# Memory attention and an erf-softplus FFN on one core: ScalarE's softplus and erf in groups of four steps, a first unit in float32, and a later split of w_out

## The chip, the cores and the metric

The kernel runs on one core of one Trainium2 chip. The metric is the device time of one execution in microseconds; lower is better. PE is TensorE, PEld its weight loads, DVE is VectorE, ACT is ScalarE, POOL is GpSimd, and SP's queue issues the transfers.

## The reference, cut to what matters

```python
# q, k, v: 8 batches x 8 heads x 576 tokens x 64; phi: 8 x 8 x 576 x 32
a = softmax(phi, axis=2)                    # over the 576 tokens
k_m = einsum('bhsm,bhsd->bhmd', a, k)       # 32 memories a head
v_m = einsum('bhsm,bhsd->bhmd', a, v)
attn = softmax(q @ k_m.T / 8, axis=-1) @ v_m
x = attn.transpose(0, 2, 1, 3).reshape(4608, 512)
h = x @ w_in                                # 512 -> 2048
sp = maximum(h, 0) + log1p(exp(-abs(h)))    # softplus
g = h * erf(sp)
return g @ w_out                            # 2048 -> 512
```

All inputs are float32. q, k and phi are scaled up, so that both softmaxes are sharp.

## The kernel before, in words

A **unit** is 288 tokens of one batch, half of its 576; there are 16. d_ff is cut into 8 **chunks** `c` of 256. A **step** `i` is one chunk of one unit, `u, c = divmod(i, 8)`: 128 steps.

The attention output is never formed. `kmvm(b, g)` makes k_m and v_m of four heads on PE, `block_diag` turns them into `km` and `vm`, and `vw(b, c)` multiplies v_m of all heads into chunk c of w_in, once per batch. `scores(u)` gives the scores, `sm_max`, `sm_norm` and `sm_back` their softmax, and `ffn1(i, j)` multiplies the attention weights `at` by the `vw` chunk, 288 tokens by 128 columns of h for each j in 0 and 1. `ffn2(i, d)` adds g of the step, times w_out's two blocks, into four accumulators `pso` of 128 columns of the output.

**Products.** Both operands of `ffn1` and `ffn2` are split into an fp32r high part and an fp32r rest (`split`: ACT copies, DVE subtracts), and three matmuls are made for each product, high x high, high x rest, rest x high (`products`). A step is 12 matmuls of `ffn1` (L390) and 24 of `ffn2` (L437), all 128 x 128 by 288.

**Activation.** h x erf(softplus(h)) is formed from Tanh alone. ACT takes `tt = tanh(0.5 h + GB)` for each j (L397), DVE multiplies (1 + tt) by h into `acc` (L398), and then `factor(i, n)` for n = 0, 1, 2 takes a Square or a Tanh of `tt` on ACT (L411, L413) and multiplies it into `acc` on DVE (L414). `g_split` makes g_hi on ACT (L422) and g_lo on DVE (L423). All functions in it, and Exp, are in one activation table.

**Weights.** w_in and w_out come as float64 bits. A piece is decoded by `decode_1` (DVE clamps, L142; ACT scales two times, L145 and L146) and `decode_2` (two passes of DVE, L159 and L162). For w_out `decode_3` splits too: ACT copies the high part (L174), PE subtracts it from the F32 value by two matmuls with the identity and its negative (L177, L178), ACT copies the rest out of PSUM (L179). Six of the eight chunks of each weight are pieces of 1 MB, the last two are pieces of half that. The decoded w_in stays in SBUF in F32, as every batch needs it for `vw`.

**Order.** `prog` is a list of calls. In front of the loop stand the first batch's attention and `LEAD` = 7 pieces of decoding. Slot i of the main loop issues `ffn1(i, 0)`, `factor(i-1, 1)`, `ffn1(i, 1)`, and then, merged, `factor(i-1, 2)`, `factor(i, 0)`, `g_split(i-2)`, the four `ffn2(i-3, d)` and the tasks in `side[i]`: in the first eight slots the decoding of two more pieces each and `vw(0, i+1)`, and everywhere the next units' and batches' attention (`unit_tasks`, `batch_tasks`), with `vw_pair` in four slots of each 16. A scheduler that simulates the engines orders each engine's instructions from this list; on DVE an instruction may not pass the one 28 places ahead of it in the list (`WINDOW`).

**Loads.** `queue` holds the loads in the order in which the program needs them; each belongs to a kind with so much `room` (buffers), `frees` gives room back, and `FIRST` sets the order of the first ones on SP's queue:

```python
FIRST = "wo phiT start phi wo raw raw wo raw start wo q".split()
```

`wo` stands for a 1 MB weight piece (in slots of the same pool as the split w_out), `raw` for k and v of a pair of heads (four transfers) or a half piece, `start` for a first-batch load in a borrowed buffer.

**Buffers.** PSUM: two for h (`ps_h`), four accumulators (`ps_o`), two for everything else (`ps_a`). SBUF: `tt` 2, `acc` 3, `f` 3, g_hi and g_lo 3 each.

Of the kernel before, what the change touches and what calls it, by code (L numbers as in the profile page):

```python
# [8 lines left out]
F32 = mybir.dt.float32  # L9
# [16 lines left out]


GC, GB = 0.27160413, -0.45239282
FACTORS = (
    ("Q", -1.75972316, 0.52065829),  # L30
    ("T", 0.56841178, 1.0199725, 0.42607248),
    ("T", 1.35008185, -1.89147316, 1.73987114),
)
# [3 lines left out]
def tile_memory_attention_then_erf_softplus_ffn(  # L37
# [3 lines left out]
    k: bass.AP,  # L41
    v: bass.AP,
# [7 lines left out]
    P = 128  # L50
    B, _, S = qT.shape
    H = k.shape[2]
# [12 lines left out]
    NF = len(FACTORS)  # L65
    SC = [(c * P, min(P, S - c * P)) for c in range((S + P - 1) // P)]
    RAW_BUFS = 3
    STAGED = 6
    FIRST = "wo phiT start phi wo raw raw wo raw start wo q".split()
    LEAD = 7  # L70
    WINDOW = {mybir.EngineType.DVE: (12, 28)}
    PO = 5
    SO = 2
    VL = 4
    VB = 1
# [18 lines left out]
    minus = const.tile([P, P], F32R, name="minus")  # L94
    nc.scalar.activation(minus, ident, AF.Identity, scale=-1.0)
# [3 lines left out]
    def column(value, name):  # L99
        t = const.tile([P, 1], F32, name=name)  # L100
        nc.vector.memset(t, value)
        return t

    tb = column(GB, "tb")
    fb = [column(f[1] if f[0] == "Q" else f[2], f"fb{i}") for i, f in enumerate(FACTORS)]
    fd = [f[2] if f[0] == "Q" else f[3] for f in FACTORS]

    w_in_sb = {}
    wo = {}

# [9 lines left out]
    def load_weight(*key):  # L120
        name, c, r, n = key
        if n == NP_:
            t = wop.tile([P, NP_ * 256], I64, name="w_" + name, tag="wo")
        else:
            t = raw_pool.tile([P, n * 256], I64, name="raw")
        if name == "in":
            nc.sync.dma_start(
                out=t.rearrange("p (r f) -> p r f", r=n),
                in_=w_in[:, r : r + n, c * 256 : (c + 1) * 256],
            )  # L130
        else:
            nc.sync.dma_start(
                out=t.rearrange("p (r d) -> p r d", d=DM),
                in_=w_out[:, 2 * c + r : 2 * c + r + n // 2],
            )
        st[key] = t
# [11 lines left out]
    def decode_2(*key):  # L148
        name, c, r, n = key
        v = st[key].bitcast(I32).rearrange("p (n two) -> p n two", two=2)  # L150
        lo, hi = v[:, :, 0], v[:, :, 1]
        dst = hi
        if name == "in":
            if r == 0:
                if c % 2 == 0:
                    w_in_sb[c // 2] = const.tile([P, NP_, 512], F32, name=f"w_in{c // 2}")
            dst = w_in_sb[c // 2].bitcast(I32)[:, r : r + n, c % 2 * 256 : (c % 2 + 1) * 256]
            hi, lo = (x.rearrange("p (r f) -> p r f", f=256) for x in (hi, lo))
        nc.vector.scalar_tensor_tensor(  # L159
# [3 lines left out]
            out=dst, in0=hi, scalar=-(2**31), in1=lo, op0=ALU.bitwise_and, op1=ALU.bitwise_or  # L163
        )

    def decode_3(*key):
        name, c, r, n = key
        t = st.pop(key)
        if name == "out":
            w = t.bitcast(F32).rearrange("p (r d two) -> p r d two", d=DM, two=2)[:, :, :, 1]  # L170
            if r == 0:
                wo[c] = wop.tile([P, 2, 2, DM], F32R, name="wo", tag="wo")
            hi, lo = (wo[c][:, x, r : r + n // 2] for x in range(2))
            nc.scalar.activation(hi, w, AF.Identity)  # L174
            for x in range(n // 2):
                ps = ps_a.tile([P, DM], F32, name="psa")
                nc.tensor.matmul(out=ps, lhsT=ident, rhs=w[:, x], start=True, stop=False)  # L177
# [11 lines left out]
    def load_phi(b):  # L189
# [6 lines left out]
        if ln < P:  # L196
            nc.sync.dma_start(out=t[:ln, n], in_=phi[b, s0 : s0 + ln])
# [446 lines left out]
```

## Time and profile before

| | |
|---|---|
| runs | 788.66, 788.80 (median), 789.77 us |
| profiled execution | 790.4 us, of which the span of the instructions is 788.5 us |
| PE, PEld busy | 750.3 us (95%), 666.4 us (85%) |
| DVE, ACT busy | 663.6 us (84%), 632.7 us (80%) |
| mean granted TensorE clock | 0.985 |
| transfers | 64.99 MB, 82 GB/s over the span |

Times inside an execution are microseconds from the start of its span. A row of a group reads: line, engine, operation, written and read tiles, shapes, count, busy time, mean ns of one, idle time of the engine just before them and what ended it. In a table by stretches the columns are PE, PEld, DVE, ACT and POOL busy with their instruction counts, then the granted clock, the transfers' share and GB/s.

### The profile page before, as it was taken

The page shows a single profiled execution, that of the slowest core. Times are in us where ns is not written, and L with a number is a line of the kernel's source. Part 1 is how long each engine was busy: PE and PEld are TensorE (multiplying, and loading weights), DVE is VectorE, ACT ScalarE, POOL GpSimd, SP SyncE. Part 2 cuts the span into 40 slices and gives each one's busy share as a digit, 9 for nine tenths or more (in the row PEclk, how much of TensorE's full clock was granted, in tenths as well). Part 3 has the DMA queues.
Part 4 walks back from the last instruction along what each step waited for, and adds up shares of the span by engine and source line. Part 5 has one row for each costly group of instructions (what it writes and reads, how often), then busy time and mean ns, then how long its engine had stood idle before and what let it go on. Part 6 is the DMA issues. An engine that isn't in the chain of part 4 may idle for free.

```text
span 788.5 us, 15764 instructions
## 1 busy us (share of the span) xinstructions
PE 750.3 (95%) x6192; PEld 666.4 (85%) x6192; DVE 663.6 (84%) x1145; ACT 632.7 (80%) x1164; POOL 0.7 (0%) x6
## 2 busy tenths in 40 slices
PE   2668899999999999999999999999999999999998
PEld 1246678789988899888988899889988899889998
DVE  4699787889979897988979798989979897889874
ACT  4699778678887878878887878878888888788784
POOL 0000000000000000000000000000000000000000
PEclk9986999999999999999999999999999999999999
DMA  9983326303060203302060203302060201100000
GB/s 275 359 316 107 86 87 171 100 1 91 13 200 1 75 18 106 106 1 91 19 193 2 76 17 109 104 1 91 18 194 1 77 1 54 40 1 31 2 31 31
DMA packets 69514, 64.99 MB, mean 82 GB/s; under 512 B 4160, under 2 KB 62016, under 8 KB 68672
## 3 DMA queue, kind: packets, MB, share of 16 engines
q1 hardware_dynamic: 69440, 63.98, 26.2%
q8 instruction: 49, 0.80, 0.4%
q14 instruction: 25, 0.20, 0.1%
HBM read 54.53 MB, written 9.44 MB: 81 GB/s over the span
## 4 chain that ended last, share of the span: by engine, by line
PE 85%; ACT 7%; DMA 5%; DVE 2%; SPq 1%; issue 1%; ACTq 0%; DVEq 0%
PE pso L437 49%; PE psh L390 25%; PE psa L308 6%; PE psa L275 3%; DMA phiT<-phiT 1%; DMA w_in<-w_in 1%; DMA raw<-k 1%; PE psa L177 1%; DMA raw<-v 1%; DVE acc L414 1%; ACT f L413 1%; ACT tt L397 1%; ACT wo L179 1%; ACT w_in L145 1%; ACT w_out L146 1%
## 5 line engine op out<-in xcount | busy, mean ns | idle before, releaser
L437 PE MATMUL pso<-g_hi,wo 128*128 128x288 f32 x2048 | 436.3, 298 | 1.0 <-ACT g_hi L422 1.0
L437 PEld LDWEIGHTS pso<-g_hi,wo 128*128 128x128 f32 x2048 | 336.7, 189 | 26.5 <-issue 13.6
L414 DVE SCALAR_TENSOR_TENSOR acc<-f,acc 128x576 f32<-128x576 f32 x384 | 289.7, 754 | 34.7 <-ACT f L411 10.6
L437 PE MATMUL pso<-g_lo,wo 128*128 128x288 f32 x1024 | 302.3, 296 | 1.0 <-DVE g_lo L423 1.0
L437 PEld LDWEIGHTS pso<-g_lo,wo 128*128 128x128 f32 x1024 | 193.7, 189 | 2.6 <-DVE g_lo L423 1.3
L413 ACT ACTIVATE f<-tt,fb 128x576 f32<-128x576 f32 x256 | 185.1, 766 | 1.9 <-DVE acc L414 1.9
L397 ACT ACTIVATE tt<-psh,tb 128x288 f32<-128x288 f32 x256 | 121.9, 497 | 44.3 <-PE psh L390 43.0
L398 DVE SCALAR_TENSOR_TENSOR acc<-tt,psh 128x288 f32<-128x288 f32 x256 | 111.1, 449 | 23.6 <-ACT tt L397 22.9
L423 DVE SCALAR_TENSOR_TENSOR g_lo<-acc,g_hi 128x576 fp32r<-128x576 f32 x128 | 96.2, 751 | 28.7 <-ACT g_hi L422 25.9
L390 PE MATMUL psh<-at_hi,vw_hi 128*128 128x288 f32 x512 | 116.2, 308 | 4.3 <-ACT at_hi L115 2.6
L422 ACT ACTIVATE g_hi<-acc 128x576 fp32r<-128x576 f32 x128 | 87.3, 682 | 39.8 <-DVE acc L414 33.7
L390 PE MATMUL psh<-at_lo,vw_hi 128*128 128x288 f32 x512 | 110.9, 298 | 0.0
L390 PE MATMUL psh<-at_hi,vw_lo 128*128 128x288 f32 x512 | 109.8, 296 | 0.0
L390 PEld LDWEIGHTS psh<-at_hi,vw_hi 128*128 128x128 f32 x512 | 82.5, 191 | 23.3 <-DVE acc L414 10.1
L411 ACT ACTIVATE f<-tt,fb 128x576 f32<-128x576 f32 x128 | 99.5, 778 | 3.1
L390 PEld LDWEIGHTS psh<-at_hi,vw_lo 128*128 128x128 f32 x512 | 83.4, 190 | 2.8 <-issue 2.4
L390 PEld LDWEIGHTS psh<-at_lo,vw_hi 128*128 128x128 f32 x512 | 83.3, 191 | 0.9 <-issue 0.8
L308 PE MATMUL psa<-w_in,vm 64*32 64x512 f32 (+1 forms) x576 | 42.6, 561 | 6.1 <-ACT wo L179 4.7
L116 DVE TENSOR_TENSOR vw_lo<-psa,vw_hi 128x512 fp32r<-128x512 f32 (+1 forms) x72 | 43.0, 624 | 1.1 <-ACT vw_hi L115 0.9
L115 ACT ACTIVATE vw_hi<-psa 128x512 fp32r<-128x512 f32 (+1 forms) x72 | 36.2, 547 | 5.8 <-PE psa L308 5.7
L453 ACT ACTIVATE ot<-pso 128x288 f32<-128x288 f32 x60 | 23.2, 402 | 12.2 <-DMA outT<-ot 11.8
L275 PE MATMUL psa<-raw,phi 128*32 128x128 f32 x620 | 28.8, 291 | 3.5 <-ACT phi L259 2.4
(73 smaller groups left out, 437.6 us busy)
## 6 DMA issues: line engine op xcount, KB each, us to landing
q<-qT SPq DMA_DIRECT2D x16, 576.0 KB, 4.2
outT<-ot SPq DMA_DIRECT2D x60, 144.0 KB, 2.5
raw<-k SPq DMA_DIRECT2D x31, 256.0 KB, 3.4
raw<-v SPq DMA_DIRECT2D x31, 256.0 KB, 3.7
w_in<-w_in SPq DMA_DIRECT2D x6, 1024.0 KB, 8.7
w_out<-w_out SPq DMA_DIRECT2D x6, 1024.0 KB, 10.2
phiT<-phiT SPq DMA_DIRECT2D x16, 288.0 KB, 4.2
phi<-phi SPq DMA_DIRECT2D x8, 512.0 KB, 5.3
```

What stands on the lines that cost most here:

```text
L116: nc.vector.tensor_tensor(out=lo, in0=src, in1=hi.bitcast(F32), op=ALU.subtract)
L275: nc.tensor.matmul(out=ps[M * j : M * (j + 1), 0, :], lhsT=a[:ln, c, (4 * g + j) * M : (4 * g + j + 1) * M], rhs=kvt[j][:ln, c], start=(c ...
L308: nc.tensor.matmul(out=ps[par][p * M : (p + 1) * M, :], lhsT=w[rows, p, :], rhs=x[rows, p, :], start=True, stop=True,)
L390: nc.tensor.matmul(out=ps, lhsT=x[:, g, j * P : (j + 1) * P], rhs=y[:, g, :], start=(k + g == 0), stop=(k == len(parts) - 1 and g == NG - 1),)
L397: nc.scalar.activation(tt[:, j], ps, AF.Tanh, bias=tb, scale=0.5)
L398: nc.vector.scalar_tensor_tensor(out=acc[:, j], in0=tt[:, j], scalar=1.0, in1=ps, op0=ALU.add, op1=ALU.mult)
L411: nc.scalar.activation(f, tt, AF.Square, bias=fb[n])
L413: nc.scalar.activation(f, tt, AF.Tanh, bias=fb[n], scale=FACTORS[n][1])
L414: nc.vector.scalar_tensor_tensor(out=acc, in0=f, scalar=fd[n], in1=acc, op0=ALU.add, op1=ALU.mult)
L422: nc.scalar.activation(hi, acc, AF.Identity, scale=GC)
L423: nc.vector.scalar_tensor_tensor(out=lo, in0=acc, scalar=GC, in1=hi.bitcast(F32), op0=ALU.mult, op1=ALU.subtract)
L437: nc.tensor.matmul(out=o, lhsT=x[:, d * P : (d + 1) * P], rhs=y[:, j, :], start=(c + j + k == 0), stop=(c == NPR - 1 and j == 1 and k == l ...
```

## The change

- **Activation.** `ffn1` ends with a DVE copy of h out of PSUM. `softplus(i)` is one ACT instruction over the step's 128 x 576. After every fourth step four `erf` follow (in place), and then four `g_split`: DVE multiplies g = erf x h, copies g_hi and subtracts for g_lo. `factor` is gone. `ffn2` comes `LAG` = 5 slots after `ffn1` instead of 3.
- **Order of tables.** Every ACT instruction whose function is not Identity, Copy or Square is tied behind the one before it in the list. `sm_exp`, `phi_exp` and `phi_sum`, cut out of `sm_max`, `phi_exp` and `phi_max`, are put at the ends of slots where a group of four ends.
- **First unit.** Steps 0 to 7 use one F32 matmul for each product: `at` of units 0 and 1 and `vw` of the first batch are not split, nor is g of the first eight steps. As unit 1 shares them, its `ffn1` is F32 as well; its `ffn2` is split.
- **w_out.** It is decoded in whole 1 MB pieces into F32 (`wf`), and `split_wo(c)` splits it in slot 8 + c, on ACT and DVE. PE's two matmuls of the split are gone. w_in's chunk c is decoded in slot c - 3, w_out's in slot c + 3; the first three of w_in before the loop.
- **Loads.** k and v come as one array, a token's k and v of two heads side by side, and a partition takes four tokens in a row: two transfers instead of four for a pair of heads. `FIRST` puts the first batch's phiT, phi, all of kv and both q behind one w_in piece and ahead of all others.
- **Buffers.** `h` 6, `e` 5, `f` 1, `phiT` 2.

The diff, cut to its core:

```diff
-GC, GB = 0.27160413, -0.45239282
-FACTORS = (
-    ("Q", -1.75972316, 0.52065829),
-    ("T", 0.56841178, 1.0199725, 0.42607248),
-    ("T", 1.35008185, -1.89147316, 1.73987114),
-)
+EVERY = (AF.Identity, AF.Copy, AF.Square)
...
-    FIRST = "wo phiT start phi wo raw raw wo raw start wo q".split()
-    LEAD = 7
-    WINDOW = {mybir.EngineType.DVE: (12, 28)}
+    FIRST = "wo phiT phiT phi raw raw raw start q start wo wo wo wo".split()
+    WINDOW = {mybir.EngineType.DVE: (40, 28)}
+    WHOLE = NPR
+    GROUP = 4
+    IN_AHEAD, OUT_AHEAD = 3, 2
+    LAG = 5
+    HB, EB = 6, 5
...
+    def split_wo(c):
+        wo[c] = wop.tile([P, 2, 2, DM], F32R, name="wo", tag="wo")
+        split(wo[c][:, 0], wo[c][:, 1], wf.pop(c))
...
+    def load_tokens(t, src):
+        n = S // P
+        ln = SC[-1][1]
+        nc.sync.dma_start(
+            out=t[:, :n], in_=src[: n * P].rearrange("(p c) e -> p c e", c=n)
+        )
+        if ln < P:
+            nc.sync.dma_start(out=t[:ln, n], in_=src[n * P :])
...
     def products(w, x):
+        if len(w) == 1:
+            return [(w[0], x[0])]
         return [(w[a], x[b]) for a, b in ((0, 0), (0, 1), (1, 0))]
...
-        nc.scalar.activation(tt[:, j], ps, AF.Tanh, bias=tb, scale=0.5)
-        nc.vector.scalar_tensor_tensor(
-            out=acc[:, j], in0=tt[:, j], scalar=1.0, in1=ps, op0=ALU.add, op1=ALU.mult
-        )
+        nc.vector.tensor_copy(out=st["h", i][:, j], in_=ps)
...
+    def softplus(i):
+        e = st["e", i] = el.tile([P, 2, U], F32, name="e", bufs=EB)
+        nc.scalar.activation(e, st["h", i], AF.Softplus)
+
+    def erf(i):
+        nc.scalar.activation(st["e", i], st["e", i], AF.Erf)
 
     def g_split(i):
-        _, acc = st.pop(("el", i))
+        g = st.pop(("e", i))
+        if i < WHOLE:
+            t = gp.tile([P, 2, U], F32, name="g", tag=("g_hi", "g_lo")[i % 2])
+            nc.vector.tensor_tensor(out=t, in0=g, in1=st.pop(("h", i)), op=ALU.mult)
+            st["g", i] = [t]
+            return
         hi = gp.tile([P, 2, U], F32R, name="g_hi")
         lo = gp.tile([P, 2, U], F32R, name="g_lo")
-        nc.scalar.activation(hi, acc, AF.Identity, scale=GC)
-        nc.vector.scalar_tensor_tensor(
-            out=lo, in0=acc, scalar=GC, in1=hi.bitcast(F32), op0=ALU.mult, op1=ALU.subtract
-        )
+        nc.vector.tensor_tensor(out=g, in0=g, in1=st.pop(("h", i)), op=ALU.mult)
+        nc.vector.tensor_copy(out=hi, in_=g)
+        nc.vector.tensor_tensor(out=lo, in0=g, in1=hi.bitcast(F32), op=ALU.subtract)
         st["g", i] = (hi, lo)
...
+    for u in range(2, NU):
+        o = start[u]
+        for n, f in ((-7, scores), (-6, sm_max), (-5, sm_exp), (-3, sm_norm), (-2, sm_back)):
+            at_slot(o + (max(n, -5) if u == 2 else n), f, u)
+    for b in range(1, B):
+        o = (b - 1) * 2 * NPR
+        e = o + (GROUP if b == 1 else 0)
         for g in range(NG):
+            at_slot(e + 1, phi_max, b, g)
+        at_slot(e + 2, phi_sub, b)
+        at_slot(e + 3, phi_exp, b)
+        for g in range(NG):
+            at_slot(e + 3, phi_sum, b, g)
+            at_slot(max(e + 4, o + 5) + g, kmvm, b, g)
+            at_slot(max(e + 5, o + 6) + g, block_diag, b, g)
         for c in range(0, NPR, 2):
+            at_slot(o + 2 * NPR - VL + c + 1, vw_pair, b, c)
...
+    for c in range(NPR):
+        need["in", c] = max(c - IN_AHEAD, -1)
+        need["out", c] = max(c + LAG - OUT_AHEAD, -1)
+        at_slot(NPR + c, split_wo, c)
...
+    for i in range(NS + LAG):
         rest = []
         if i < NS:
+            prog += [(ffn1, i, 0), (ffn1, i, 1)]
+            rest = [(softplus, i)]
+            if i % GROUP == GROUP - 1:
+                rest += [(erf, i - GROUP + 1 + x) for x in range(GROUP)]
+                rest += [(g_split, i - GROUP + 1 + x) for x in range(GROUP)]
+        if i >= LAG:
+            rest = merge([(ffn2, i - LAG, d) for d in range(NDM)], rest)
+        if i < NS:
+            rest = merge(rest, [x for x in side[i] if x[0] not in late])
+            rest = merge(rest, decode[i])
+            rest += [x for x in side[i] if x[0] in late]
...
+            if isinstance(x, mybir.InstActivation) and x.func not in EVERY:
+                if last is not None:
+                    tc.add_manual_dep(x, last.name, near, reason="table order")
+                last = x
```

353 lines of the change are left out of this document (151 added, 202 removed).

## The prediction

> **What bounds the kernel now.** I read four views in this order: the page's slices, the busy time in stretches cut at the loop's own steps, the groups of instructions of the stretch that looked different, and the instructions in order of time. "Slot i" is the pass of the main loop that issues `ffn1(i, 0)`; `L390` is the matmul of `ffn1`, `L437` that of `ffn2`, each step having 12 and 24 of them.
>
> The page, engine shares and slices of 19.7 us:
>
> ```profile
> PE 750.3 (95%) x6192; PEld 666.4 (85%) x6192; DVE 663.6 (84%) x1145; ACT 632.7 (80%) x1164; POOL 0.7 (0%) x6
> ...
> PE   2668899999999999999999999999999999999998
> ```
>
> PE is full from the sixth slice to the end, and not in the first five. So there are two regimes, and a share of the whole span says nothing about the first. The stretches below are cut where unit 0's `scores` starts (30.24), where slot 0 starts (45.98), at slot 8 (123.03), slot 11 (138.79), and then at slots 32 and 64:
>
> ```profile
> 0.00:30.24 30.24, 9.68 (x88) 5.52 (x88) 13.59 (x25) 15.90 (x27) 0.70 (x6) 1.00 0.94 290
> 30.24:45.98 15.74, 10.13 (x46) 3.37 (x45) 14.96 (x21) 13.46 (x22) 0.00 (x0) 0.97 1.03 404
> 45.98:123.03 77.05, 69.19 (x432) 52.03 (x433) 67.94 (x122) 66.20 (x115) 0.00 (x0) 0.85 0.41 131
> 123.03:138.79 15.76, 15.76 (x173) 13.59 (x171) 12.11 (x20) 14.57 (x35) 0.00 (x0) 1.00 0.59 165
> 138.79:253.96 115.17, 115.17 (x965) 102.55 (x963) 101.03 (x177) 92.66 (x172) 0.00 (x0) 1.00 0.23 68
> 253.96:430.37 176.41, 176.19 (x1528) 161.19 (x1521) 153.47 (x269) 144.51 (x272) 0.00 (x0) 1.00 0.23 68
> ```
>
> Columns: stretch and length; PE, PEld, DVE, ACT and POOL busy (instructions); granted clock; DMA share; GB/s. After slot 11, 32 slots take 176.4 us, 5.51 each, with PE busy throughout. That PE is at its limit there and not only called busy shows in the chain that ended last, where 24 matmuls of `ffn2` take 3.17 us, 132 ns each:
>
> ```profile
> 284.17 3.17 PE pso L437 x24
> ```
>
> 36 x 0.132 = 4.75 us of each 5.51 are the FFN, and vw, scores and kmvm fill most of the rest. Of what PE waits for, the largest row that the activation causes is small:
>
> ```profile
> PEld psh L390 <- DVE acc L414: 10.1, 16, 0.8
> ```
>
> 10.1 us in the whole run, in weight loads that mostly lie beside matmuls. A lighter activation can win little there. From 30.24 to slot 11, 108.55 us, DVE is busy 14.96 + 67.94 + 12.11 = 95.0 us (87.5%) and ACT 13.46 + 66.20 + 14.57 = 94.2 us (86.8%): both nearly full with weight decoding and the first steps' activation. PE runs there at a reduced clock. So the start is set by DVE and ACT, the rest by PE, and I cost the change as three terms: when `scores(0)` starts, how long from there to slot 11, and what PE has left at slot 11.
>
> **Term 1: the first loads.** In time order, before:
>
> ```profile
> 4.52 0.69 SPq L132 DMA_DIRECT2D w_out<-w_out  x1
> ...
> 14.70 0.57 SPq L127 DMA_DIRECT2D w_in<-w_in  x1
> ...
> 25.68 0.43 PE L275 MATMUL psa<-kv,phi 128*32 128x128 f32 x2 [0.93 <-DMA kv<-v]
> ```
> ```profile
> 30.24 2.35 PE L308 MATMUL psa<-q,km 64*32 64x288 f32 x16
> ```
>
> The second kmvm waits for the last kv until 25.68, and scores follows at 30.24. On SP's queue a w_out piece (1.05 MB) goes ahead of every k and v, and a w_in piece (1.05 MB) ahead of half of them. The new order puts the first w_in, phiT, phi, all kv and both q first. 2.1 MB at the 290 GB/s of the first stretch is 7.2 us: scores at about 23. Eight issues for kv take the place of sixteen; SP's own 0.5 to 0.7 us each lie under the transfers (DMA 94% busy), so I count nothing; if the transfers became quicker, SP's eight or so microseconds for these issues would show next. Bounds: 30 if something else holds scores, 20 if the longer rows also move faster. I take 23, nearest to the row with the rate.
>
> **Term 2: from scores to slot 11.** DVE and ACT groups of that stretch (30.24 to 138.79) before; last columns are busy us and mean ns:
>
> ```profile
> L414 DVE SCALAR_TENSOR_TENSOR acc<-f,acc 128x576 f32<-128x576 f32 x32 | 24.1, 753 | 2.3 <-ACT f L411 0.7 <-DVE acc L414 0.5
> L398 DVE SCALAR_TENSOR_TENSOR acc<-tt,psh 128x288 f32<-128x288 f32 x22 | 9.4, 448 | 3.6 <-ACT tt L397 3.5
> L423 DVE SCALAR_TENSOR_TENSOR g_lo<-acc,g_hi 128x576 fp32r<-128x576 f32 x10 | 7.6, 756 | 4.8 <-ACT g_hi L422 4.7
> L116 DVE TENSOR_TENSOR vw_lo<-psa,vw_hi 128x256 fp32r<-128x256 f32 x16 | 6.4, 416 | 0.2
> L159 DVE SCALAR_TENSOR_TENSOR w_out<-w_out 128x1024 int32<-128x1024 int32 x5 | 6.1, 1222 | 2.0 <-ACT w_out L146 2.0
> ...
> L142 DVE TENSOR_SCALAR w_out<-w_out 128x1024 f32<-128x1024 f32 x4 | 2.8, 690 | 0.0
> ```
> ```profile
> L413 ACT ACTIVATE f<-tt,fb 128x576 f32<-128x576 f32 x22 | 16.1, 783 | 0.0
> L397 ACT ACTIVATE tt<-psh,tb 128x288 f32<-128x288 f32 x22 | 10.1, 511 | 1.3 <-PE psh L390 1.3
> L179 ACT ACTIVATE wo<-psa 128x512 fp32r<-128x512 f32 x16 | 9.5, 600 | 4.8 <-PE psa L178 4.8
> L411 ACT ACTIVATE f<-tt,fb 128x576 f32<-128x576 f32 x11 | 8.7, 790 | 0.1
> L422 ACT ACTIVATE g_hi<-acc 128x576 fp32r<-128x576 f32 x10 | 6.9, 692 | 0.5 <-DVE acc L414 0.5
> ...
> L174 ACT ACTIVATE wo<-w_out 128x1024 fp32r<-128x1024 f32 x5 | 5.9, 1180 | 0.1
> ...
> L174 ACT ACTIVATE wo<-raw 128x512 fp32r<-128x512 f32 x4 | 2.7, 671 | 1.5 <-PE psa L177 1.5
> ```
>
> DVE loses the three factor passes (24.1), g_lo (7.6) and vw_lo of the first unit pair (6.4). The copy `h<-psh` takes the place of L398 one for one, at 0.36 (its 0.45 without the second input's wait) to 0.48; I leave 0.45. It gains: eight multiplies g = e x h of 128x576, at 0.753 as the other two-input passes: 6.0. Two more decoded pieces fall into the stretch (15 instead of 13, as w_out 0 and w_in 1 went back behind the attention), 2 x (0.69 + 2 x 1.22) = 6.3. Three `split_wo` at slots 8 to 10, one subtract over 1024 columns each, at the 1.22 of L159: 3.7. DVE: 95.0 - 38.1 + 16.0 = 72.9 us.
>
> ACT loses L413, L397, L179, L411, L422 and both L174: 59.9 us. It gains eleven softplus and eight erf of 128x576. No row shows either; ACT's rows of that shape run 0.69 (L422) to 0.79 (L411), and I take 0.783, the one nearest in kind: 14.9. Two decoded pieces, two passes over 1024 columns each at L174's 1.18: 4.7. Three split copies at 1.18: 3.5. And the table switches. One is in the trace:
>
> ```profile
> L95 ACT ACT_TABLE_LOAD x1 | 1.3, 1283 | 0.7 <-PEq L634 0.7
> ```
>
> By order Exp, softplus, erf, softplus, erf, Exp, softplus there are six up to slot 8 if the three functions have three tables, four if Exp shares one. Bounds: nothing (all in one) to 1.28 each on an idle engine plus what a busy one must first finish, at most one 0.79 instruction. I take 6 x 1.283 = 7.7. ACT: 94.2 - 59.9 + 30.8 = 65.1 us.
>
> The Trainium skill, "ScalarE: Activation LUTs", section What ACT_TABLE_LOAD costs, gives 1283 ns for the load and about 1380 ns of drain with it, 2.66 us a switch. The trace agrees on the first number; its one load came on an idle engine and shows no drain. By the Trainium skill ACT would have 8.3 us more, 73.4, and the stretch would be 73.4/0.868 = 84.6 us, 1.3 more than below.
>
> DVE stays the fuller one. At before's 87.5% it takes 72.9/0.875 = 83.3 us, so slot 11 starts at 23 + 83 = 106. Bounds: 72.9 if DVE never waits, 104 if it is 70% busy. I take before's share, since the chain decode, activation, matmul is of the same kind.
>
> PE must also fit. `L177` and `L178` split w_out on PE before: an F32 pair and an fp32r matmul, from 81.16 to the next matmul at 82.29:
>
> ```profile
> 81.16 1.06 PE L177 MATMUL psa<-w_out,ident 128*128 128x512 f32 x2
> 81.64 0.81 PE L178 MATMUL psa<-wo,minus 128*128 128x512 f32 x1
> 82.29 0.30 PE L390 MATMUL psh<-at_hi,vw_lo 128*128 128x288 f32 x1
> ```
> ```profile
> 263.67 1.09 PE L308 MATMUL psa<-w_in,vm 64*32 64x512 f32 x16
> ```
>
> That is 1.13 us, 16 times, and all of it goes: 18 us. The fp32r one at 132 ns per 288 columns is 0.235, so F32 costs 0.90 per 512 columns, 0.50 per 288. A first-unit step then is 4 + 8 F32 matmuls, 6.0 us instead of 4.75. Unit 1 shares the unsplit `at` and `vw`, so its `ffn1` too is four F32 matmuls, 2.0 instead of 1.6. Up to slot 11 PE has eleven `ffn1` of 2.0, six F32 `ffn2` of 4.0, and some 10 for ten groups like the last row's, about 1 us each (vw, scores, kmvm): 56 us at full clock. In 83 us there is room down to a clock of 0.67.
>
> **Term 3: after slot 11.** Before it was 788.5 - 138.8 = 649.7. With a lag of 5 instead of 3, steps 6 and 7 are still owed to `ffn2`, in F32: + 8.0. The five F32 `ffn1` of slots 11 to 15 add 5 x 0.42 = 2.1: 659.8. The steady step stays PE's. DVE per 16 slots: 153.47/2 = 76.7, less 16 x (3 x 0.753 + 0.756), plus 16 x (0.753 + copy g_hi + 0.753). That copy has no row; one-input passes in SBUF run 0.69 per 1024 columns (L142), two-input ones 0.75 per 576, so 0.4 to 0.75, and 0.46 is nearest. It comes to 60 of 88 us. ACT: 144.51/2 = 72.3 less 16 x 4.07 (L413 twice, L397 twice, L411, L422), plus 32 x 0.78 and ten switches of 1.28: 45 of 88. The five later `split_wo` (2.4 us on both engines together, slots 11 to 15) fit into that. `sm_exp` and the phi exponentials now queue behind the four erf at the end of their slot; what waits for them, `sm_norm` and kmvm, is placed one or two slots later, so nothing by that.
>
> The new wait is the group: g of step 4k needs softplus(4k+3), a switch, erf and three DVE passes, 0.45 + 0.78 + 1.28 + 0.78 + 1.97 = 5.3 us after `ffn1(4k+3)`. `ffn2(4k)` comes after one and a half slots, some 9 us. Queued behind it are the `h` copies; they have a slot before PE wants their bank. I cost it at nothing; its cover is those 4 us. At the end two more `ffn2` stand before the last group, 6.3 us against the same chain: nothing.
>
> **Sum.** 23 + 83.3 + 659.8 = 766.1 of span, against 788.5: 22.4 less. The profiled execution took 790.4 in all, 1.9 more than its span; the runs' median is 788.8, and 22.4 less than that is 766.4.
>
> **The rivals.** *The start does not get denser* (0.15): groups of four bring the first g late, and in-order table switches and PE at half clock keep DVE at 70 to 75%. Then slot 11 comes 14 to 21 later: 780 to 787. For it speaks the clock, which fell wherever PE had gaps:
>
> ```profile
> 40.00:60.00 20.00, 13.94 (x85) 7.85 (x83) 18.98 (x28) 19.97 (x31) 0.00 (x0) 0.80 0.79 300
> 60.00:80.00 20.00, 16.72 (x78) 13.23 (x79) 20.00 (x33) 18.68 (x29) 0.00 (x0) 0.69 0.33 106
> ```
>
> Against it: DVE and ACT were full in just these rows.
>
> *PE becomes the start's bound* (0.03): at a clock of 0.5 throughout, 56 us become 112, and 23 + 112 + 659.8 = 795. It takes the lead below 0.67 and undoes the whole gain at 0.53; 0.69 is the lowest in 20 us of the trace. The Trainium skill, "TensorE: Matmul & The Clock Gate", section What's actually happening, says that an idle window of some 3.4 us halves the clock and a busy one restores it; by that rule a PE that has become the bound is busy and recovers, against this rival.
>
> *Slower, by the groups* (0.10): in the steady state each group lets PE stand, because ACT has evictions of vw, kvk or exponentials ahead of the erf, so the 4 us of cover are used up. From slot 12 there are 29 groups; 22.4/29 = 0.77 us per group undoes the gain. At 1.2 us it is 766 + 35 = 801. Against it: ACT would be half idle.
>
> *More* (0.13): DVE waits for almost nothing at the start (72.9) or the psh waits above go, or both: 750 to 759.
>
> **How the numbers follow.** My own case holds 0.59, 759 to 777. Faster by over 0.2% (about 1.6 us, what a measurement can tell here from no change): 0.59 + 0.15 + 0.13 = 0.87; within, half of PE's case and a little: 0.02; slower 0.11. From 753 to 783 the two slow cases are left out (0.13) and the ends of two others (some 0.06).
>
> **What would show it.** Scores at 20 to 26 and slot 11 near 106, with DVE the fuller of the two; no `L177`; F32 matmuls of `ffn1` 0.5 apart; about 80 table loads; 16 slots still 88 us; PE without waits for g. Wrong it would be if 16 slots took over 90 us, or if slot 11 came after 120.

## The result, and the profile after

| | before | after |
|---|---|---|
| median of four runs | 789.28 us (788.66 to 790.63) | 820.24 us (818.61 to 821.19) |
| profiled execution, span | 790.4, 788.5 us | 820.3, 818.5 us |
| scores(0), slot 11, end of span | 30.24, 138.79, 788.5 | 25.05, 116.11, 818.5 |
| transfers | 64.99 MB | 64.88 MB |

The ratio is 1.0388 (95% interval 1.0365 to 1.0410): the kernel became 3.9% slower, where 766 us were predicted. One execution of e1 below (1896.8 us) and one of e4 (2579.1 us) took more than twice as long as the others of the same kernel; the medians here leave them out, and as e1's one profile is of that execution, no busy time of e1 is given.

The page after, engine shares and slices of 20.5 us:

```profile
PE 772.7 (94%) x6016; PEld 653.8 (80%) x6016; DVE 520.5 (64%) x975; ACT 431.9 (53%) x702; POOL 0.7 (0%) x6
...
PE   2468999999999999999999999999999999999998
...
DVE  3788939674557656665676755576566645667553
ACT  3759775465453745445364754537454563446351
```

DVE lost 143 us and ACT 201 us, as the change intends. PE has 176 instructions fewer and is busy for 22 us more. That is the first sign: of the 30 us that the span grew by, 22 went into PE's own work and not into waiting. The stretches, cut at scores(0), slot 11, slot 32, slot 48, slot 64 and the end:

```profile
25.05:116.11 91.06, 69.99 (x433) 42.41 (x432) 73.45 (x106) 68.52 (x97) 0.00 (x0) 0.83 0.57 210
116.11:244.09 127.98, 126.93 (x958) 105.83 (x955) 83.97 (x161) 68.10 (x114) 0.00 (x0) 1.00 0.23 70
244.09:339.92 95.83, 94.55 (x769) 81.63 (x761) 59.95 (x118) 48.78 (x83) 0.00 (x0) 1.00 0.20 63
339.92:435.34 95.42, 94.48 (x768) 81.65 (x760) 59.95 (x118) 48.77 (x83) 0.00 (x0) 1.00 0.19 63
435.34:818.50 383.16, 378.53 (x3032) 337.44 (x3024) 236.09 (x458) 188.64 (x309) 0.00 (x0) 1.00 0.14 44
```

The start brought its gain (slot 11 is 22.7 us earlier), and everything behind it lost 52.7 us: 702.4 us from slot 11 to the end instead of 649.7. Sixteen slots take 95.8 us instead of 88.2, with PE busy for 94.55 of them at full clock.

Which of PE's instructions grew, is seen when the groups are kept apart by shape. First before, then after:

```profile
L308 PE MATMUL psa<-w_in,vm 64*32 64x512 f32 x448 | 32.6, 601 | 0.0
L308 PE MATMUL psa<-q,km 64*32 64x288 f32 x256 | 19.0, 431 | 0.0
```
```profile
L294 PE MATMUL psa<-w_in,vm 64*32 64x512 f32 x448 | 56.4, 601 | 0.0
L294 PE MATMUL psa<-q,km 64*32 64x288 f32 x256 | 23.3, 441 | 1.6 <-ACT km L281 1.3 <-ACT vw L316 0.3
```

The same 448 records of `vw` (two for each F32 matmul), each of the same mean duration, 601 ns, cover 56.4 us instead of 32.6. A mean of 601 ns times 448 would be 269 us: these matmuls use 64 rows and 32 columns of the array and lie on top of each other, and the busy time is their union. So they lie on top of each other less. PE's instructions in order of time, at the slot where it is worst; records on one line were issued behind one another:

```profile
319.72 0.29 PE L434 MATMUL pso<-g_hi,wo 128*128 128x288 f32 x1
319.94 1.04 PE L294 MATMUL psa<-w_in,vm 64*32 64x512 f32 x2
320.92 0.53 PE L388 MATMUL psh<-at_hi,vw_hi 128*128 128x288 f32 x2
...
322.04 1.05 PE L294 MATMUL psa<-w_in,vm 64*32 64x512 f32 x4
323.01 0.40 PE L434 MATMUL pso<-g_hi,wo 128*128 128x288 f32 x1
323.34 1.05 PE L294 MATMUL psa<-w_in,vm 64*32 64x512 f32 x4
324.32 0.40 PE L434 MATMUL pso<-g_lo,wo 128*128 128x288 f32 x1
...
328.20 1.05 PE L294 MATMUL psa<-w_in,vm 64*32 64x512 f32 x6
329.18 0.53 PE L388 MATMUL psh<-at_hi,vw_hi 128*128 128x288 f32 x2
```

One `heads` of `vw_pair`, eight matmuls, stands in four groups of 1, 2, 2 and 3 with `ffn1` and `ffn2` between them, and each group occupies PE for 0.97 to 0.98 us, however many matmuls are in it. The Trainium skill, "TensorE: Matmul & The Clock Gate", section Measured speedup vs the span model, states the same as a rule: the span of packed tiles is one matmul's duration plus some 4 ns for each further tile. The trace agrees in kind, with another figure: further records of a group start about 7 ns apart here. And it shows the other side of that rule: a group that is cut in four costs four durations. The full-array matmuls between the groups cost more as well: the single `ffn2` matmul at 323.01 holds PE for 0.33 us until the next group starts, where one in an unbroken run takes 0.13.

What ACT did in the same slot:

```profile
313.00 0.69 ACT L403 ACTIVATE e<-h 128x576 f32<-128x576 f32 x1 [3.79 <-DVE h L395]
313.71 1.28 ACT L406 ACT_TABLE_LOAD   x1
315.00 2.41 ACT L406 ACTIVATE e<-e 128x576 f32<-128x576 f32 x4
317.43 1.28 ACT L343 ACT_TABLE_LOAD   x1
318.72 0.69 ACT L343 ACTIVATE sc<-sc 128x576 f32<-128x576 f32 x1
319.44 0.71 ACT L458 ACTIVATE ot<-pso 128x288 f32<-128x288 f32 x2
321.73 0.41 ACT L458 ACTIVATE ot<-pso 128x288 f32<-128x288 f32 x1 [1.58 <-DMA outT<-ot]
322.16 1.28 ACT L403 ACT_TABLE_LOAD   x1
323.45 0.68 ACT L403 ACTIVATE e<-h 128x576 f32<-128x576 f32 x1
324.04 0.39 ACT L458 ACTIVATE ot<-pso 128x288 f32<-128x288 f32 x1
```

`ot` is the copy of the four accumulators at the end of a unit; the first `ffn2` of the next unit (`L434`) can't start before it. It stands behind the erf group, two table loads and the Exp of `sm_exp`; then, as there are two `ot` buffers, behind a store; then behind a third load and a softplus. In the order that the scheduler laid down for PE, the `vw` matmuls are dealt out over that time, so that PE itself waits for these copies for only 4.2 us in the whole run:

```profile
PE pso L434 <- ACT ot L458: 4.2, 9, 1.0
```

I had not named these copies in the prediction.

### The profile page after: what moved, and what is told of

The parts are those of the page before. It is cut to its first block, busy times and chain, and to the rows that moved or that the text cites. A ratio compares the mean times of both kernels' runs of the same rounds, so it can differ in the third digit from the quotient of the medians.

```text
span 818.5 us, 14277 instructions
## 1 busy us (share of the span) xinstructions
PE 772.7 (94%) x6016; PEld 653.8 (80%) x6016; DVE 520.5 (64%) x975; ACT 431.9 (53%) x702; POOL 0.7 (0%) x6
## 2 busy tenths in 40 slices
DMA packets 34367, 64.88 MB, mean 79 GB/s; under 512 B 3072, under 2 KB 22016, under 8 KB 33280
## 4 chain that ended last, share of the span: by engine, by line
PE 77%; ACT 11%; DVE 6%; DMA 4%; SPq 1%; issue 1%; ACTq 0%
PE pso L434 43%; PE psh L388 23%; PE psa L294 7%; PE psa L261 3%; ACT e L406 2%; DMA outT<-ot 2%; DMA w_in<-w_in 1%; ACT L406 1%; ACT phiT L239 1%; DMA kv<-kv 1%; DVE phi L229 1%; ACT L343 1%; ACT e L403 1%; ACT vw_hi L102 1%; ACT phi L251 1%
## 5 line engine op out<-in xcount | busy, mean ns | idle before, releaser
L434 PE MATMUL pso<-g_hi,wo 128*128 128x288 f32 x1920 | 407.5, 296 | 4.3 <-ACT ot L458 4.2
L434 PEld LDWEIGHTS pso<-g_hi,wo 128*128 128x128 f32 x1920 | 314.7, 188 | 18.5 <-ACT ot L458 12.7
L434 PE MATMUL pso<-g_lo,wo 128*128 128x288 f32 x960 | 283.8, 297 | 0.6 <-DVE g_lo L419 0.6
L403 ACT ACTIVATE e<-h 128x576 f32<-128x576 f32 x128 | 87.9, 687 | 235.2 <-DVE h L395 234.9
L395 DVE COPY h<-psh 128x288 f32<-128x288 f32 x256 | 114.4, 452 | 124.0 <-PE psh L388 123.4
L434 PEld LDWEIGHTS pso<-g_lo,wo 128*128 128x128 f32 x960 | 180.3, 188 | 10.2 <-DVE sc L352 5.0
L417 DVE TENSOR_TENSOR e<-e,h 128x576 f32<-128x576 f32 x120 | 88.0, 754 | 83.1 <-ACT e L406 83.1
L388 PE MATMUL psh<-at_hi,vw_lo 128*128 128x288 f32 x448 | 95.8, 295 | 0.0
L388 PEld LDWEIGHTS psh<-at_hi,vw_hi 128*128 128x128 f32 x448 | 70.4, 188 | 28.9 <-issue 11.6
L419 DVE TENSOR_TENSOR g_lo<-e,g_hi 128x576 fp32r<-128x576 f32 x120 | 90.0, 752 | 0.9
L406 ACT ACTIVATE e<-e 128x576 f32<-128x576 f32 x128 | 77.3, 675 | 0.4
L418 DVE CAST g_hi<-e 128x576 fp32r<-128x576 f32 x120 | 54.7, 456 | 32.1 <-PE pso L434 31.3
L388 PE MATMUL psh<-at,vw 128*128 128x288 f32 x128 | 40.2, 451 | 14.8 <-DVE at L360 12.1
L102 ACT ACTIVATE vw_hi<-psa 128x512 fp32r<-128x512 f32 x56 | 30.2, 588 | 36.4 <-PE psa L294 36.4
L388 PEld LDWEIGHTS psh<-at,vw 128*128 128x128 f32 x128 | 24.4, 204 | 27.9 <-DVE at L360 13.0
```

What stands on the lines that cost most here:

```text
L102: nc.scalar.activation(hi, src, AF.Identity)
L388: nc.tensor.matmul(out=ps, lhsT=x[:, g, j * P : (j + 1) * P], rhs=y[:, g, :], start=(k + g == 0), stop=(k == len(parts) - 1 and g == NG - 1),)
L395: nc.vector.tensor_copy(out=st["h", i][:, j], in_=ps)
L403: nc.scalar.activation(e, st["h", i], AF.Softplus)
L406: nc.scalar.activation(st["e", i], st["e", i], AF.Erf)
L417: nc.vector.tensor_tensor(out=g, in0=g, in1=st.pop(("h", i)), op=ALU.mult)
```

## The experiments

Fourteen kernels ran. All but e12 start from the changed kernel; "term 3" is the span from slot 11 to the end. The ratio is to the kernel before on the same chip; that kernel took 789.3 to 791.4 us on the chips used, so differences between the medians of two rows are good to some 2 us. The last two columns are PE's busy time in the 448 records of `vw` and, counted in the order of PE's instructions, the groups in which they stand.

| | median us | ratio, 95% interval | vw us | groups |
|---|---|---|---|---|
| changed kernel | 820.24 | 1.0388 (1.0365 to 1.0410) | 56.4 | 53 |
| e1_no_switch | 808.02 | 1.0235 (1.0185 to 1.0284) | | 53 |
| e2_lag6 | 792.43 | 1.0032 (1.0011 to 1.0053) | 30.5 | 28 |
| e3_lag4 | 833.29 | 1.0541 (1.0507 to 1.0574) | 30.5 | 28 |
| e4_ot_buffers | 811.33 | 1.0259 (1.0226 to 1.0292) | 56.4 | 53 |
| e5_lag6_ot4 | 772.59 | 0.9783 (0.9754 to 0.9812) | 30.5 | 28 |
| e6_halves_apart | 775.02 | 0.9815 (0.9785 to 0.9846) | 30.5 | 28 |
| e7_old_activation | 778.72 | 0.9854 (0.9828 to 0.9880) | 31.5 | 29 |
| e8_old_places | 817.66 | 1.0346 (1.0318 to 1.0374) | 38.8 | 36 |
| e9_halves_far | 806.08 | 1.0189 (1.0165 to 1.0213) | 58.5 | 55 |
| e10_lag5_ot_dve | 803.26 | 1.0145 (1.0108 to 1.0182) | 44.0 | 41 |
| e11_lag6_ot4_dve | 777.44 | 0.9832 (0.9799 to 0.9865) | 30.5 | 28 |
| e12_before_ot4 | 787.07 | 0.9948 (0.9924 to 0.9973) | 31.5 | 29 |
| e13_vw_a_slot_earlier | 798.38 | 1.0101 (1.0057 to 1.0144) | 30.5 | 28 |
| e14_vw_earlier_ot4 | 792.92 | 1.0025 (1.0001 to 1.0049) | 30.5 | 28 |

Wherever a busy time is given, it is 1.06 to 1.09 us for each group. My theory was that the late accumulators break up the packed matmuls; the rivals, that the table loads do the harm, or that the chain to g does.

**The table loads.**

```diff
-        nc.scalar.activation(e, st["h", i], AF.Softplus)
+        nc.scalar.activation(e, st["h", i], AF.Tanh)
...
-        nc.scalar.activation(st["e", i], st["e", i], AF.Erf)
+        nc.scalar.activation(st["e", i], st["e", i], AF.Tanh)
```

> The changed kernel with Tanh in the place of softplus and of erf (so g is another function of h); Tanh shares Exp's table, so that no table is switched in the loop, and PE's order of instructions stays the same, 53 runs of vw matmuls of 512 columns included. Theory A (the time went into vw, scores and kmvm matmuls that PE issues in pieces, and into waits for the accumulators): the pieces stay; only the waits behind table loads go, 5 to 10 us: 810 to 816. Theory B (table switches hold up the activation chain and so PE): about 32 us go, 785 to 790.

Measured 806.84, 808.02 and 813.04: by the median 12 us less than the changed kernel, 2 us below theory A's range and 18 above theory B's. The loads have a price, somewhat under a quarter of the 53.9 us by which the changed kernel missed the predicted time. As only three executions count, it is known to a few us.

**The lag.**

```diff
-    LAG = 5
+    LAG = 6
```

> The changed kernel with LAG = 6 instead of 5: ffn2 of a unit ends and the next unit's begins one slot later, no longer in the slot right behind the erf group and the exponentials. PE's order then has the 224 vw matmuls in 28 unbroken runs of 8 instead of 53 pieces, scores in 18 instead of 30, kmvm in 19 instead of 30. Theory A: 25 pieces x 1 us, 12 x 0.5 and 11 x 0.5, and part of some 10 us of waits: 775 to 785; 16 slots at 88 to 90 us. Theory B (table switches): as many switches, the same chain: 815 to 820.

Measured 792.43, 27.8 us less than the changed kernel, and 7 more than theory A allows; theory B is out. The groups are whole, but a new wait has come, shown here by the waits of PE, and by SP's queue and PE in order of time:

```profile
PE psa L261 <- DMA kv<-kv: 16.2, 6, 3.2
```
```profile
272.37 5.44 SPq L461 DMA_DIRECT2D outT<-ot  x4
277.90 0.38 SPq L173 DMA_DIRECT2D kv<-kv  x1
```
```profile
281.75 1.42 PE L261 MATMUL psa<-kv,phi 128*32 128x128 f32 x36 [2.42 <-DMA kv<-kv]
```

SP issues in order: the kv loads stood for 5.4 us behind four stores that waited for ACT's `ot` copies, and kmvm waited for kv. In e5 below, which has more `ot` buffers as well, the same four stores take 3.3 us. A lag of 4 instead of 6:

```diff
-    LAG = 5
+    LAG = 4
```

> LAG = 4: the unit's end falls into the slot of the erf group itself, ahead of it, and PE's order again has vw in 28 unbroken runs of 8, scores in 25, kmvm in 18. Theory A: close to LAG = 6, 780 to 790, if g comes in time; its first g of a group has one slot less, so up to 29 groups x 0.5 us may be added. Theory C (the lag of the groups is what is too short, PE waits for g): slower than the changed kernel, 825 to 840.

Measured 833.29, in theory C's range and the slowest of all, though the groups of `vw` are whole. PE's waits:

```profile
PE pso L434 <- ACT ot L458: 16.2, 13, 1.7
PE pso L434 <- DVE g_lo L419: 15.6, 20, 1.6
```

At a lag of 4 g itself is late. So the chain to g is a real limit, only it is reached at 4; in the changed kernel PE's matmuls wait for g_lo for 0.6 us in the whole run.

**The buffers.**

```diff
-    ost = ctx.enter_context(tc.tile_pool(name="ost", bufs=2))
+    ost = ctx.enter_context(tc.tile_pool(name="ost", bufs=4))
```

> Four buffers for output tiles instead of two, LAG = 5: ACT no longer waits for an output transfer before it can free an accumulator. The vw matmuls stay in 53 pieces, kmvm comes in 24 instead of 30. Theory A: only the waits for the transfer go, up to 12 us and 3 us of kmvm: 806 to 815. Theory D (the output transfer's wait is the root of all): 785 to 790.

Measured 811.33, 8.9 us less, in theory A's range. In the changed kernel ACT's copies waited 17.7 us for the stores, and here they no longer do; the rows are those of the changed kernel and of e4:

```profile
L458 ACT ACTIVATE ot<-pso 128x288 f32<-128x288 f32 x60 | 22.7, 405 | 22.1 <-DMA outT<-ot 17.7 <-PE pso L434 4.0
```
```profile
L458 ACT ACTIVATE ot<-pso 128x288 f32<-128x288 f32 x60 | 21.2, 403 | 4.9 <-PE pso L434 4.7
```

**Both**, LAG 6 and four buffers:

```diff
-    LAG = 5
+    LAG = 6
...
-    ost = ctx.enter_context(tc.tile_pool(name="ost", bufs=2))
+    ost = ctx.enter_context(tc.tile_pool(name="ost", bufs=4))
```

> LAG = 6 and four buffers for output tiles. With LAG = 6 alone PE waited 16 us in seven kmvm for kv, whose transfer was issued behind the four output stores, and these behind accumulator copies that waited for the buffer of an earlier store. Theory A (broken runs of matmuls, waits for accumulators and what follows in SP's queue): the waits for kv fall to a few us; 16 slots at 88 to 89 us; 775 to 783. Rival: the kv transfer itself is late, whatever stands before it: 789 to 793, as with LAG = 6 alone.

Measured 772.59: faster than both kernels, and 47.6 us below the changed one, which is more than the two edits' 27.8 and 8.9 together, as the buffers also take away e2's wait for kv (16.2 to 3.6 us). Slot 11 comes at 113.02, term 3 is 658.2 us, and 16 slots take 87.4 us (32 to 48) and 88.2 us (48 to 64); the first stretch and slots 32 to 48 are:

```profile
24.90:113.02 88.12, 67.30 (x396) 41.54 (x396) 74.05 (x107) 68.83 (x96) 0.00 (x0) 0.98 0.59 218
231.10:318.53 87.43, 87.13 (x768) 80.42 (x760) 59.98 (x119) 48.56 (x83) 0.00 (x0) 1.00 0.22 69
```

**Order within a group.** e5 with the lower row halves of `heads` first, then the upper ones:

```diff
-        for p in range(NP_):
-            for par in range(2):
+        for par in range(2):
+            for p in range(NP_):
```

> As LAG = 6 with four output buffers, but vw and scores issue the four matmuls of the lower 64 rows first and then the four of the upper 64, instead of in turns: the same matmuls in the same 28 and about as many unbroken runs. Theory A (PE works such matmuls at the same time only where neighbours in its order use other parts of the array, so a piece costs nearly as much as a whole run): each vw run takes nearly twice its 1.02 us, each scores run nearly twice 0.65: 28 x 0.9 + 16 x 0.5 = 33 us more than the kernel with LAG = 6 and four buffers. Rival (matmul count sets the price): the same time within 3 us.

Measured 775.02, with 30.5 us for `vw` as in e5. My expectation was wrong, and the rival's 3 us held: within an unbroken group the order of the tiles costs `vw` nothing. Whether the number of matmuls sets the price, as the rival says, or the number of groups, e9 then tested.

**Groups cut on purpose.** e5 with each `vw_pair` cut into its row halves, called one slot apart:

```diff
...
-            at_slot(o + 2 * NPR - VL + c + 1, vw_pair, b, c)
+            at_slot(o + 2 * NPR - VL + c, vw_half, b, c, 0)
+            at_slot(o + 2 * NPR - VL + c + 1, vw_half, b, c, 1)
```

> The kernel of e5_lag6_ot4 (LAG 6, four buffers for ot; 772.59 us), with each pair's vw cut into its two row halves and the first half called one slot earlier than the second: 55 groups of vw matmuls of 512 columns in PE's list order instead of 28, nearly all of half the size, and six more groups of scores. Theory A (a group's time on PE does not depend on its size, 0.97 us for a part against 1.02 us for a whole one): 27 x 0.97 + 6 x 0.6 = 30 us more, 800 to 806, and two half groups cost 1.95 us together in the profile. Theory B (a matmul of vw has its own price of 1.02/8 and the groups only came late): 770 to 776, and a half group costs 0.5 us.

Measured 806.08: 33.5 us more than e5 (the expectation's upper end, 806). PE's rows of e5, then of e9:

```profile
L294 PE MATMUL psa<-w_in,vm 64*32 64x512 f32 x448 | 30.5, 601 | 0.0
L294 PE MATMUL psa<-q,km 64*32 64x288 f32 x256 | 15.9, 448 | 1.2 <-ACT km L281 0.9 <-ACT vw L316 0.3
```
```profile
L294 PE MATMUL psa<-w_in,vm 64*32 64x512 f32 x448 | 58.5, 601 | 0.0
L294 PE MATMUL psa<-q,km 64*32 64x288 f32 x256 | 19.8, 448 | 1.5 <-ACT km L281 1.3 <-ACT vw L316 0.3
```

28.0 and 3.9 us more of PE: 31.9 of the 33.5. PE's idle time is 3 us less than in e5, no work is added, and the lag and the buffers are those of the fast kernel. The number of matmuls is the same, so it doesn't set the price, and theory B is out. The price of a broken group is thus shown, apart from any lateness.

**Is it the cause at LAG 5?** Two kernels first left it open. e8 puts the attention's steps into the slots of the kernel before:

```diff
-        for n, f in ((-7, scores), (-6, sm_max), (-5, sm_exp), (-3, sm_norm), (-2, sm_back)):
-            at_slot(o + (max(n, -5) if u == 2 else n), f, u)
+        m = -5 if u % 2 == 0 else -6
+        for n, f in ((0, scores), (1, sm_max), (1, sm_exp), (2, sm_norm), (3, sm_back)):
+            at_slot(o + m + n, f, u)
...
-            at_slot(max(e + 4, o + 5) + g, kmvm, b, g)
-            at_slot(max(e + 5, o + 6) + g, block_diag, b, g)
...
+            at_slot(o + 8 + g, kmvm, b, g)
+            at_slot(o + 9 + g, block_diag, b, g)
...
-    late = (sm_exp, phi_sum, phi_exp)
+    late = ()
```

> The changed kernel, LAG = 5, softplus and erf in groups of four, with the attention tasks (scores, softmax, phi, kmvm) in the slots that they had before. PE's order then has vw in 36 pieces instead of 53, scores in 18 instead of 30, kmvm in 19 instead of 30. Theory A: 17 pieces x 1 us, 12 x 0.5, 11 x 0.5, some waits: 785 to 793. Rival (the groups' latency holds PE up): 812 to 820.

Measured 817.66, in the rival's range. The broken groups fell (38.8 us of `vw`), but waits came in their place; in the changed kernel the first and the third were 1.2 and 4.2 us, and the second did not occur:

```profile
PE psa L277 <- ACT kvk L269: 8.5, 8, 1.2
PE psa L261 <- DMA kv<-kv: 8.0, 5, 2.0
PE pso L434 <- ACT ot L458: 7.5, 6, 1.3
```

e10 keeps LAG 5 and copies `ot` on DVE, with four buffers:

```diff
-    ost = ctx.enter_context(tc.tile_pool(name="ost", bufs=2))
+    ost = ctx.enter_context(tc.tile_pool(name="ost", bufs=4))
...
-            nc.scalar.activation(t, o, AF.Identity)
+            nc.vector.tensor_copy(out=t, in_=o)
```

> The changed kernel at its LAG of 5, with the accumulators ot of even units copied out by DVE instead of ACT, and four buffers for them; 41 groups of vw instead of 53, scores as before with 30. Theory A (at LAG 5 the accumulators come late because they queue on ACT behind the erf group and its table loads): the copies no longer hold PE; what stays is 12 groups fewer and the waits behind ot gone, of 39 us about 25: 785 to 798. Theory B (at LAG 5 it is g itself, the chain of softplus, erf and split, that comes too late): 806 to 815, no better than with the four buffers alone (811.34), and PE waits for g_lo.

The edit moves the copies of all units (60 of `ot` in the trace), not only of even ones. Measured 803.26, between the two theories. `vw` still stands in 41 groups (44.0 us), `scores` in 30 (23.3 us); against e5 that is 13.5 and 7.4 of the 30.7 us. ACT's queue is thus only a part of what breaks the groups.

What decides is the place. At LAG 5 the first `ffn2` of a unit falls into slots 5 mod 8, and one of the four `vw_pair` of a batch is called in such a slot, 13 mod 16. In PE's order these calls make 19 of the 25 groups that the changed kernel has more than e5. The other six come from the pair called in slot 3 mod 16, cut in two halves between that slot and the next, where a unit's last `ffn2` stands. Why the scheduler cut them in just these slots no trace shows. e13 (two buffers) and e14 (four) call each `vw_pair` one slot earlier, and change nothing else:

```diff
-    VL = 4
+    VL = 5
```

> The changed kernel at its LAG of 5 with its two buffers for ot, and each vw_pair called one slot earlier (VL 5 for 4), so that none is called in the slot in which the first ffn2 of a unit waits for its accumulators: 28 groups of vw of 512 columns in PE's list instead of 53, scores as before with 30, kmvm in 42 groups instead of 30. Theory A (what the changed kernel lost is mostly the price of the broken groups of vw): PE's time on these matmuls falls from 56.4 to 30.5 us, kmvm takes some 2 us more, and the time is 820 less 24: 794 to 799. Theory B (broken groups only fill time in which PE would wait for the accumulators and g): the vw matmuls fall as well, but the waits for ot and g grow by as much, and the time is 812 to 820.

> The same with four buffers for ot. Theory A: 811.34 (four buffers alone) less 24: 785 to 790. Theory B: 804 to 811.

Measured 798.38 and 792.92: 21.9 us less than the changed kernel and 18.4 less than e4. `vw` falls to 30.5 us in both. e13 lies in theory A's range, e14 3 us above it; theory B's ranges begin 14 and 11 us higher. PE's row of e13:

```profile
L294 PE MATMUL psa<-w_in,vm 64*32 64x512 f32 x448 | 30.5, 601 | 0.0
```

e14 still lies 20 us above e5. `scores` has 23.8 us for 15.9, and kmvm, now in 42 groups, 36.8 for 29.8: 15 of the 20. The rest stays open.

**Two controls.** e7 is the changed kernel with the activation, the LAG of 3 and the attention's slots of the kernel before, so with the new loads, the first unit in F32 and the late split alone:

```diff
...
-    LAG = 5
+    LAG = 3
...
+            nc.scalar.activation(f, tt, AF.Tanh, bias=fb[n], scale=FACTORS[n][1])
...
```

> All of the change but the activation and the order of the attention tasks: product of factors from Tanh without groups, LAG = 3, attention tasks in the slots of the kernel before; float32 first unit, later split of w_out and the new loads stay. PE's order has vw in 29 runs. Theory A: 16 slots at 88 to 89 us as before; the start keeps most of its gain, slot 11 at 118 to 124 against 138.8 before and 116.1 in the changed kernel: 770 to 778. Rival (the start's gain is the lighter activation's): slot 11 after 130, 783 to 790.

Measured 778.72, 0.7 us above theory A's range. Behind slot 11 it takes 648.7 us, like the kernel before (649.7); so what the changed kernel lost there came with the activation, its lag and the attention's slots. Slot 11 comes at 127.06, later than I expected: 11.7 of the 22.7 us gained up to slot 11 come from loads, F32 and split. The other 11 come with the activation and its lag, and not all of them are a gain: at a lag of 5 two F32 `ffn2`, 8.0 us of PE by the prediction's price, are still owed at slot 11, which e7 has done by then. The best kernel with softplus and erf (e5, with two more `ot` buffers) is 6 us ahead of e7, which itself is 11.6 us below the kernel before on its chip: of e5's 17.7 us the larger part is there without the new activation.

e12 is the kernel before with four `ot` buffers:

```diff
-    ost = ctx.enter_context(tc.tile_pool(name="ost", bufs=2))
+    ost = ctx.enter_context(tc.tile_pool(name="ost", bufs=4))
```

> The kernel before with four buffers for ot instead of two: how much of the gain of e5_lag6_ot4 is due to the buffers alone. 29 groups of vw instead of 30, 23 of scores instead of 25. Theory A (before, ACT's copies came early enough, and two buffers were enough): 786 to 791. Theory B (the buffers help any version): 778 to 785.

Measured 787.07, in theory A's range; but that range was set from the first runs' 789, and against the kernel before on the same chip it is 0.5% faster, with an interval that excludes no change. The buffers are worth about 4 us there, so e5's gain over the kernel before is not just theirs.

e11 is e5 with `ot` on DVE:

```diff
-            nc.scalar.activation(t, o, AF.Identity)
+            nc.vector.tensor_copy(out=t, in_=o)
```

> The kernel of e5_lag6_ot4, with ot copied by DVE. The groups on PE are as in e5 (28 of vw, 19 of scores for 18). Theory A (with LAG 6 nothing waits for ACT's copies any more): 769 to 775, the same as 772.59. Theory B (the copies on ACT still hold PE at the first ffn2 of a unit): 762 to 769.

Measured 777.44, 5 us slower than e5 and outside both ranges: with LAG 6 nothing is gained by taking the copies off ACT. In its profiled execution (780.7 us) slot 11 came 3 us later than in e5's and the rest took 5 us more; which of DVE's instructions are delayed is open. e5 is the best version.

## Why the prediction was wrong, point by point

- **Term 1, scores at 23:** 25.05. Within its bounds, 2 us later than the value taken.
- **Term 2, 83.3 us to slot 11:** 91.06. The amounts were right: DVE 73.45 us (72.9 predicted), ACT 68.52 (65.1). The share was not: 81% of DVE instead of 87.5%. Three stretches show why, two on either side of the first `ffn2` at 75.35, and the last slots of the start:

```profile
55.00:75.35 20.35, 15.81 (x121) 7.81 (x120) 19.27 (x30) 18.35 (x31) 0.00 (x0) 0.92 0.74 308
75.35:95.00 19.65, 19.65 (x83) 15.26 (x77) 16.23 (x21) 17.82 (x20) 0.00 (x0) 0.91 0.00 1
97.07:116.11 19.04, 18.25 (x140) 12.49 (x139) 9.27 (x18) 13.77 (x24) 0.00 (x0) 1.00 0.30 94
```

  DVE and ACT were nearly full, as predicted, until the first g existed. From then on PE was full, with all the owed F32 `ffn2` to do, and DVE fell to 83% and then to 49%. The prediction compared PE's work with the whole stretch, and did not ask how much of it can't begin before 75.35. The reduced clock behind 52 us was a small part. The profile's clock column can't show that by itself: in the changed kernel, e4 and e5 alike, `vw` matmuls of 256 columns last some 630 ns at 30 to 35 us and 388 ns later, but the column has 0.50 there in the changed kernel and 1.00 in e4 and e5, whose traces hold no record of the clock so early. After 52 us e4 shows no reduced clock, the changed kernel two stretches of 3.4 us. e4's extra buffers are first used behind slot 11, and it took 88.55 us from scores to slot 11; so these two stretches are worth at most 2.5 of the 7.8 us.
- **Term 3, 659.8 us after slot 11:** 702.4. This step failed, and its sentence is "The steady step stays PE's", with 16 slots at 88 us. PE did stay the bound, but its work was not the fixed sum I took it for. The sum took over the kernel before's 649.7 us with the groups of `vw`, `scores` and kmvm as they were ("about 1 us each" in term 2), though the change moves the lag, the accumulators' copies and the attention's slots, on which the number of groups depends. It had 16 slots over 90 us as a sign of being wrong, and they took 95.8.

  Against the kernel before, `vw` grew by 23.8 and `scores` by 4.3 us: 28 of the 42.6 us missing. For `vw` the runs show it both ways: e13 makes the groups whole and saves 21.9 us, e9 cuts whole ones and loses 33.5. Four `ot` buffers are worth 8.9 (e4).

  Counted from the start of each of PE's matmul records to the start of the next, from slot 11 on, so that nothing counts twice, the missing time is, within 0.2 us, 22.2 us in `vw`, 3.0 in `scores`, 3.6 in kmvm and its transposes, 4.0 of PE standing idle, and 10.0 in `ffn1` and `ffn2` beyond the 10.1 that the sum had added for F32. e9 shows a part of the last: counted in this way it has 33 more groups than e5, and 5.7 us more in `ffn1` and `ffn2`, whose unbroken runs the groups interrupt (the 0.33 us for 0.13 above). The changed kernel has some 36 groups more than the kernel before, which would be 6 of the 10.0; the other 4 stay open.

  With whole groups and four buffers term 3 is 658.2 (e5). That this lies 1.6 us from the prediction is partly luck: at LAG 6 a third F32 `ffn2` is owed at slot 11, 4.0 us more by the prediction's price, and e5's `vw` and `scores` take 5.2 us less than those of the kernel before.
- **What I costed at nothing.** "So nothing by that", said of the Exp queueing behind erf, was wrong for an instruction I hadn't looked at: `ot` queues behind both. g itself was as predicted, hidden by its cover at LAG 5 (PE's matmuls wait 0.6 us for g_lo); at LAG 4 it isn't (e3).
- **Durations.** softplus and erf took 0.69 and 0.68 us (0.783 taken), the copy to g_hi 0.456 (0.46), `h<-psh` 0.452 (0.45), an F32 matmul over 288 columns, which is two records, 0.49 (0.50; four records of `ffn1` take from 84.42 to 85.39). DVE's steady amount was 59.95 us (60), ACT's 48.8 (45). There were 80 table loads. No load had more than its own 1.28 us: softplus ended at 313.69, the load began at 313.71, erf at 315.00. The Trainium skill, "ScalarE: Activation LUTs", section What ACT_TABLE_LOAD costs, adds a drain of some 1.4 us to each load; this trace shows none.
- **The rivals.** "The start does not get denser" came true in part: slot 11 was 10 us late, with DVE at 81% and not at 70 to 75, and less by the clock than by PE's late work. Its rows on the clock are to be read with care, too: the column has 1.00 up to 30.24, where PE was busy for 9.68 us alone, but the matmuls of `scores` at 30.24 last some 683 ns, and 415 at 90 us. "Slower, by the groups" had the right sign, given 0.10, and the wrong mechanism: it had ACT's evictions ahead of erf; in fact erf and the loads stood ahead of an eviction, and PE hardly stood (4.9 us idle from slot 11 on, 0.8 before) but worked badly. Four slots cost (95.8 - 88.2) / 4 = 1.9 us more where it had 1.2.

## What to carry to other kernels

Where small matmuls share the array, cost them by groups and not by number: whatever lets a scheduler slip a full-array matmul between them adds a whole duration (0.97 us here), and PE will look full, not waiting. When an edit lengthens one engine's queue, list everything on that engine that frees a PSUM bank, the rare copies at the end of a loop too, and see what else is placed in the slot where they are due. An engine that is busier with fewer instructions is the sign to look for, and the shapes kept apart with their summed durations against the busy time show it.

## What the runs showed of the hardware that was not expected

- F32 matmuls of 64 rows by 32 columns with a 512-column moving side: one to three in a group occupy PE for 0.97 to 0.98 us (the changed kernel), four for 0.99 (e9), eight for 1.02 (two rows of e5; start to next start):

```profile
230.08 1.09 PE L294 MATMUL psa<-w_in,vm 64*32 64x512 f32 x16
231.10 0.53 PE L388 MATMUL psh<-at_hi,vw_hi 128*128 128x288 f32 x2
```

  The order of the tiles within the group makes no difference (e6).
- Softplus, erf and Exp needed three different tables: 32 loads before softplus, 32 before erf, 14 before Exp of the softmax in the loop.
- A store that waits for its data holds every load behind it on the same queue: four stores held SP for 5.44 us in e2, and PE waited 16.2 us for kv in the whole run; with four buffers PE's wait is 3.6 us (e5).
